# Adding the skip term inside PSUM: a seed matmul ahead of the kernel sums in place of a GpSimd addition

## The chip, the cores and the metric

The kernel runs on one core of a Trainium2 chip. The metric is the device time of one launch in microseconds (us), as the median of several runs. The engines have short names in the profile: PE is TensorE (PEld its weight loads), DVE is VectorE, ACT is ScalarE, POOL is GpSimd, SP is SyncE. A q behind a name (SPq, ACTq, POOLq) is that engine's sequencer, which also issues DMAs.

## The reference

The input `A_u` has 2048 tokens of 448 channels. With `xn` its layer norm, the output is `A_u + A(xn) + B(xn)`.

- `A` is a diagonal state space layer. From five small parameter arrays it builds for each channel d a convolution kernel `K[d, l] = 2 Re sum_n C[d,n] exp(A[d,n] dt[d] l)` over 256 states n and 2048 positions l, convolves `xn` with it through transforms of length 4096, and adds the skip term:

```
y = irfft(rfft(u_t, 2L) * rfft(K, 2L))[:, :, :L]
return y + u * D_skip
```

- `B` is a gated unit: `(sigmoid(xn w_gate) * (xn w_up)) w_down`, 448 to 1792 and back.

A skip term `u * D_skip` is the same as adding `D_skip[d]` to the first tap `K[d, 0]` of the convolution kernel. The kernel uses that, before and after the change.

## The kernel before, in words

Two generators, `conv()` and `glu()`, issue the two halves of the work piece by piece; each `yield` returns a weight, and the loop at the end of the kernel resumes the one that is further behind its total. The program order that comes out is a priority, not yet the order on the engines. `TileContext(schedule_with_timeline_sim=True)` plays the program against a model of the chip ahead of the launch, and puts on each engine's queue the ready instruction of the highest priority; `hp(HP)` raises the priority of what is under it and `tc.issue_after(x)` keeps an instruction behind `x` on its engine. On the chip each queue then runs in that fixed order.

**The gated unit** (`gate`, L689, and `glu`, L724) splits each fp32 operand into a high and a low fp32r part. A tile of 128 hidden units takes 11 matmuls (L703) each for gate and up; the down projection (L816) takes three matmuls for each hidden tile and block of tokens. Weight parts `wh`, `wl` and `dh`, `dl` are made by ACT and DVE in the first half (L753 to L757, L779) with `dl` by POOL (L780); in the second half some are made by POOL (L763, L764, L787, L788). The first `wl` (L755) reads a column of the small tile `lim`, which POOL sets in `limits` (L174 to L176) behind the layer norm's scales.

**The convolution** goes in stages. `prep` (L341) turns the parameters into phases and powers with ACT and DVE. `kgen` (L457) makes the convolution kernel in 56 chunks of 8 channels. For a chunk, POOL builds magnitudes `me` and `mf` by repeated products (`magnitudes`, L493, called for two chunks at a time; L504, L516), ACT squares some of them (L529) and makes cosines and sines `S` (`ahead`, L531) out of a phase matmul (L538), DVE multiplies both into `Et` and `Ft` (L598 to L600), and PE sums over the states with 32 small fp32 matmuls (L612, two passes each in the trace), each into 32 rows and 64 columns of the PSUM tile `ko`.

Four chunks fill one `ko` bank, so there are 14 banks. `ko` has a single buffer. Behind the fourth chunk ACT copies the bank to `ks` in SBUF (L622), and POOL adds the skip weights `dm` to the columns that hold tap 0 (L623). Three chunks later, or at once for the last bank, `first_stage` (L550) multiplies `ks` with a table (L562) and stores the result for `spectra`. In `ko` the four 32-row groups j hold four channels of a slot, and row 32 j, column 0 of slot s holds tap 0; `dm` is therefore zero but for rows 0, 32, 64 and 96, which four small loads fill at the start (L1066, L1067). POOL takes its queue strictly in order, so an addition that waits for its copy keeps the magnitudes behind it waiting too.

`spectra` (L838) then transforms, multiplies and transforms back, beside the second half of the gated unit.

Of the kernel before, what the change touches and what calls it, by code (L numbers as in the profile page):

```python
# [11 lines left out]
F32 = mybir.dt.float32  # L12
F32R = mybir.dt.float32r
I32 = mybir.dt.int32
AF = mybir.ActivationFunctionType
ALU = mybir.AluOpType
# [4 lines left out]
D = 448  # L21
# [34 lines left out]
def _tables():  # L56

    a = np.arange(NA)[:, None]
    k1 = np.arange(NK1)[None, :]
    ang = 2 * np.pi * ((a * k1) % 64) / 64.0  # L60


    wk = np.zeros((4, NA, 2, 2, 32))

    wx = np.zeros((4, NA, 64))
    for j in range(4):
        wk[j, :, 0, j % 2] = np.cos(ang)[:, :32]
        wk[j, :, 1, j % 2] = -np.sin(ang)[:, :32]
        wk[j, :, 1, j % 2, 0] = np.cos(ang)[:, 32]
        wx[j, :, :NK1] = np.cos(ang)  # L70
        wx[j, :, NK1:] = -np.sin(ang)[:, 1:32]
    b = np.arange(NB)[:, None]
    k2 = np.arange(64)[None, :]
    tab = np.zeros((NK1, 128, 128))
    bk = np.zeros((2, 2, 64, 2, 128))
    for q in range(NK1):
        al = 2 * np.pi * ((b * (q + 64 * k2)) % 4096) / 4096.0
        c, s = np.cos(al), np.sin(al)
        tab[q] = np.block([[c, -s], [s, c]])
        if q in (0, 32):  # L80


            for h in range(2):

                split = lambda t: t.reshape(64, 2, 32).transpose(0, 2, 1)
                both = lambda r, i: np.stack([split(r), split(i)], 3).reshape(64, 128)
                bk[q // 32, h, :, 0] = both(c.T, s.T)
                bk[q // 32, h, :, 1] = both(-s.T, c.T)

    tab[0, 64:] = 0.0  # L90
    t32 = np.concatenate([tab[32][:, None], bk[1].reshape(128, 2, 128)], 1)
    tab = tab[:32].reshape(8, 4, 128, 128).transpose(0, 2, 1, 3)

    wf = np.zeros((2, 2, 4, 8, 32, NA))
    for k in range(32):
        ang = 2 * np.pi * ((k * (64 * np.arange(NA)[None] + np.arange(64)[:, None])) % 4096) / 4096.0
        re = (1.0 if k == 0 else 2.0) / 4096.0 * np.cos(ang)
        im = -2.0 / 4096.0 * np.sin(ang)
        if k == 0:
            im = np.broadcast_to(np.cos(np.pi * np.arange(NA))[None] / 4096.0, im.shape)  # L100
        wf[:, 0, k % 4, k // 4] = re.reshape(2, 32, NA)
        wf[:, 1, k % 4, k // 4] = im.reshape(2, 32, NA)

    sel = np.zeros((4, 32, 2, DC, 32))
    st = np.arange(32) + 0.5
    for e in range(DC):
        g, r = e // 2, 6 * (e % 2)  # L110
        for at, sg in ((r, 1.0), (r + 14, -1.0)):
            sel[g, at : at + 2, 0, e] = sg * st
            sel[g, at + 2 : at + 4, 1, e] = sg * st
            sel[g, at + 4 : at + 6, 1, e] = sg
        sel[g, 12, :, e] = MAGIC
        sel[g, 13, :, e] = -MAGIC
    f = lambda v, s: np.ascontiguousarray(v.reshape(s).astype(np.float32))
    return {
        "c_wk": f(wk, (128, 2, 64)),
        "c_wx": f(wx, (128, 64)),  # L120
        "c_tab": f(tab, (8, 128, 4, 128)),
        "c_t32": f(t32, (128, 3, 128)),
        "c_bk": f(bk[0], (128, 2, 128)),
        "c_wf": f(wf, (128, 32, NA)),
        "c_sel": f(sel, (128, 512)),
        "c_id": np.eye(128, dtype=np.float32),
    }

# [2 lines left out]
def s4d_glu_kernel(ctx, tc, io):  # L131
    nc = tc.nc
# [18 lines left out]
    const = ctx.enter_context(tc.tile_pool(name="const", bufs=1, side="left"))  # L151
# [8 lines left out]
    qpi = const.tile([128, 1], F32, name="qpi")  # L160
    nc.gpsimd.memset(qpi, math.pi / 4)

    dm = const.tile([128, D // 32, 8], F32, name="dm")
    nc.gpsimd.memset(dm, 0.0)
    ys = const.tile([128, 16], F32, name="ys")
    zs = const.tile([128, 16], F32, name="zs")
    junk = const.tile([128, 1], F32, name="junk")
# [277 lines left out]
    def powers(pms, g, behind=None):  # L445

        w = W1s[0][:, NCH * g : NCH * g + NCH].rearrange("p g h e -> p (g h e)")
        pm = pms[g % 2]
        with tc.issue_after(behind.ins) if behind else nullcontext():
            nc.scalar.activation(pm[:, 0], w, AF.Identity, bias=one)  # L450
        for j in (1, 2, 3, 4, 5, 7, 8, 9, 10, 11):
            v.scalar_tensor_tensor(pm[:, j], w, 2.0, w, ALU.add, ALU.mult)
            w = pm[:, j]
        for o in (slice(1, 6), slice(7, 12)):
            nc.scalar.activation(pm[:, o], pm[:, o], AF.Identity, bias=one)

    def kgen(pk):  # L457
# [73 lines left out]
        def ahead(cn):  # L531


            S = tl[f"S{cn % 2}"]
            ps = psc[-1].tile([128, 2, 512], F32, name="tr", bufs=1)
            ph = pht[cn // 2 % 2]
            for h in range(2):
                nc.tensor.matmul(ps[:, h], ph[:, cn % 2, 128 * h : 128 * h + 128], sel, start=True, stop=True)  # L538
            if cn % 2 == 1 and cn + 3 < NCK:
                phase_load(cn // 2 + 2)  # L540
            rows = lambda t: t.rearrange("p c (h e) s -> p h c (e s)", h=2)
            pv = ps.rearrange("p h (c x) -> p h c x", c=2)
            cs = S[:, 1:4:2]
            nc.scalar.activation(rows(cs), pv, AF.Abs)  # L544
            nc.scalar.activation(rows(S[:, 0:5:4]), pv, AF.Sin, scale=TWO_PI)
            nc.scalar.activation(rows(S[:, 2:3]), pv[:, :, 0:1], AF.Sin, scale=-TWO_PI)
            sins[:] = [nc.scalar.activation(cs, cs, AF.Sin, scale=-TWO_PI, bias=hpi)]  # L547
            return S
# [33 lines left out]
        for g in range(NCK // NCH):  # L582
            for c in range(NCH):
                cn = g * NCH + c
                S = nxt
                me, mf = (m[:, 2 * DC * (c % 2) : 2 * DC * (c % 2) + 2 * DC] for m in mags)
                if c == 4 and NCH * (g + 1) < NCK:
                    with tc.issue_after(fts[0].ins):
                        powers(pms, g + 1, sins[0])
                if cn + 1 < NCK:  # L590
                    nxt = ahead(cn + 1)
                    if c % 2 == 1:
                        squares(coming[0])
                yield WK / 2
                Et = tl[f"Et{cn % 2}"]
                Ft = tl["Ft"]
                two = lambda ap: ap.unsqueeze(1).to_broadcast([128, 2, 2 * DC, 32])
                v.tensor_tensor(Et[:, :, :, 32:64], two(me[:, :, 32:64]), S[:, 1::-1], ALU.mult)  # L598
                v.tensor_tensor(Et[:, :, :, 0:32], two(me[:, :, 0:32]), S[:, 1:3, :, ::-1], ALU.mult)  # L599
                fts[:] = [v.tensor_tensor(Ft, two(mf), S[:, 3:5], ALU.mult)]  # L600
                if cn + 2 < NCK and c % 2 == 0:
                    coming = magnitudes(cn // 2 + 1)
                if c % 2 == 1:
                    mags = coming
                if cn % 4 == 0:
                    ko = psc[-1].tile([128, 8, 64], F32, name="ko", bufs=1)
                for q in range(2):
                    sl = 2 * (cn % 4) + q
                    for k in range(4):
                        h, cc = k // 2, k % 2  # L610
                        for j in range(4):
                            mm = nc.tensor.matmul(  # L612
                                ko[32 * j : 32 * j + 32, sl],
                                Ft[:, cc, DC * h + 4 * q + j],
                                Et[:, cc, DC * h + 4 * q + j],
                                start=(k == 0),
                                stop=(k == 3),
                                skip_group_check=True,
                            )
                if cn % 4 == 3:  # L620
                    ks = tl["ks"]
                    nc.scalar.copy(ks, ko)  # L622
                    nc.gpsimd.tensor_tensor(ks[:, :, 0], ks[:, :, 0], dm[:, cn // 4], ALU.add)  # L623
                yield WK / 2
                if cn % 4 == 2 and cn > 3 or cn + 1 == NCK:

                    with hp(HP) if cn + 1 == NCK else tc.issue_after(glu_mm[0].ins):
                        first_stage((cn - 3) // 4 if cn + 1 < NCK else cn // 4)
# [387 lines left out]
    def conv():  # L1016
        with tc.tile_pool(name="psk", bufs=1, space=PSUM) as ps_, tc.tile_pool(
            name="pq", bufs=1, side="right"
# [8 lines left out]
            with tc.tile_pool(name="pst", bufs=1, side="right", reuse_waits="tile") as pst:  # L1027
# [35 lines left out]
                nc.sync.dma_start(wk, io["c_wk"])  # L1063
                nc.sync.dma_start(wx, io["c_wx"])
                skip = io["A_D_skip"].rearrange("(g s j) -> j g s", j=4, s=8)
                for j in range(4):  # L1066
                    nc.gpsimd.dma_start(dm[32 * j : 32 * j + 1], skip[j : j + 1])  # L1067
                preps = [prep(pst, h, srcs[h]) for h in range(2)]

                with tc.issue_after(xls[0].ins):  # L1070
# [44 lines left out]
    while any(g is not None for g in gens):  # L1115
# [3 lines left out]
        i = min(live, key=lambda i: done[i] / total[i])  # L1119
# [33 lines left out]
```

## Time and profile before

| | |
|---|---|
| median of 3 runs | 725.41 us (724.01 to 725.96) |
| profiled execution, device time | 727.18 us |
| its span | 725.4 us |
| granted TensorE clock, mean | 0.984 |
| busy: PE, DVE, ACT, POOL | 669.3, 558.1, 428.4, 365.7 us |

The span runs from the first to the last instruction of the profiled execution; the device time has 1.8 us more around it. Busy times are sums over a queue and say nothing about what a stage waits for. A line of a timeline has the start in us, the time that one instruction (or a run of equal ones) took, the engine, the line of the code, the operation, output and input tiles, and in brackets how long the engine had been idle and what ended that. In a table of groups the number behind x is the count, then come busy us and mean ns of one, then the idle time ahead of them. Matmuls are pipelined: the next one starts while the one before still drains, so the cost of one is read from start to start.

### The profile page before, as it was taken

The numbers are of one execution on the slowest core, as the hardware profiler recorded it, in microseconds if no ns is written. First come the engines' busy times: TensorE is split into PE (matmuls) and PEld (weight loads), VectorE is DVE, ScalarE is ACT, GpSimd is POOL, SyncE is SP. The second block draws the span as 40 slices with busy tenths as digits, with TensorE's granted clock in tenths as the row PEclk, the third lists the DMA queues.
The fourth block names the chain that finished last, engine by engine and source line by source line (L and its number), as shares of the span: only waits on it lengthen the run. The fifth ranks groups of instructions, "written<-read, shape, count | busy, mean of one in ns | idle before, by whom it ended". The sixth has DMA issues, their size and how long they took to land.

```text
span 725.4 us, 19184 instructions
## 1 busy us (share of the span) xinstructions
PE 669.3 (92%) x7752; PEld 525.6 (72%) x7752; DVE 558.1 (77%) x766; ACT 428.4 (59%) x678; POOL 365.7 (50%) x431
## 2 busy tenths in 40 slices
PE   2797999999997996998999999999999999998995
PEld 2666888887876873656788778887777787666783
DVE  5899897599899889897878888987946555545543
ACT  3655975578788777975777777777642322312320
POOL 2100138566987975796666688577843002250001
PEclk9999999999999998999999999999999999999998
DMA  9957184454254443656833334141369999999745
GB/s 205 238 142 226 38 253 141 149 166 148 67 168 141 133 121 111 173 147 200 256 101 101 98 110 147 45 143 42 82 173 321 231 238 225 247 263 215 183 121 160
DMA packets 102984, 117.24 MB, mean 162 GB/s; under 512 B 13232, under 2 KB 90864, under 8 KB 102896
## 3 DMA queue, kind: packets, MB, share of 16 engines
q1 hardware_dynamic: 78736, 91.87, 46.9%
q10 hardware_dynamic: 21584, 18.24, 9.4%
q0 software_dynamic: 2576, 5.90, 3.0%
q8 instruction: 61, 1.00, 0.6%
q14 instruction: 27, 0.22, 0.1%
HBM read 72.13 MB, written 43.84 MB: 160 GB/s over the span
## 4 chain that ended last, share of the span: by engine, by line
PE 63%; DVE 13%; DMA 8%; ACT 6%; issue 4%; SPq 3%; POOL 2%; ACTq 0%; POOLq 0%; DVEq 0%
PE gu L703 27%; PE po L816 14%; PE sp L898 7%; PE ko L612 6%; PE pv L925 4%; PE tr L538 4%; DVE Ft L600 2%; DVE Et L598 2%; DMA sx<-x_d 2%; DVE Et L599 2%; DMA ph<-ph_d 1%; PE kp L562 1%; DMA xe<-in_A_u_dram 1%; ACT S L547 1%; DVE hl L721 1%
## 5 line engine op out<-in xcount | busy, mean ns | idle before, releaser
L516 POOL TENSOR_TENSOR me<-me,pm 128x32 f32<-128x32 f32 (+1 forms) x168 | 141.6, 843 | 77.7 <-DVE Et L599 66.7
L516 POOL TENSOR_TENSOR mf<-mf,pm 128x64 f32<-128x64 f32 (+1 forms) x112 | 116.5, 1040 | 5.9
L703 PE MATMUL gu<-xh,wh 128*128 128x512 f32 x336 | 98.6, 401 | 1.6 <-ACT xh L221 0.7
L703 PE MATMUL gu<-xh,wl 128*128 128x512 f32 x336 | 96.0, 391 | 0.0
L703 PE MATMUL gu<-xl,wh 128*128 128x512 f32 x336 | 95.5, 390 | 0.0
L598 DVE TENSOR_TENSOR Et<-me,S 128x1024 f32<-128x1024 f32 x56 | 84.5, 1509 | 13.7 <-ACT S L547 12.8
L816 PE MATMUL po<-dh,hh 128*128 128x448 f32 x224 | 84.3, 377 | 6.3 <-DVE hf L714 4.4
L599 DVE TENSOR_TENSOR Et<-me,S 128x1024 f32<-128x1024 f32 x56 | 79.2, 1414 | 11.4 <-ACT me L529 9.3
L600 DVE TENSOR_TENSOR Ft<-mf,S 128x1024 f32<-128x1024 f32 x56 | 79.5, 1420 | 6.4 <-PE ko L612 3.3
L816 PE MATMUL po<-dl,hh 128*128 128x448 f32 x224 | 82.7, 369 | 0.0
L816 PE MATMUL po<-dh,hl 128*128 128x448 f32 x224 | 81.7, 368 | 0.0
L544 ACT ACTIVATE S<-tr 128x1024 f32<-128x1024 f32 x56 | 57.6, 1029 | 38.7 <-PE tr L538 38.4
L612 PEld LDWEIGHTS ko<-Et,Ft 128*32 128x32 f32 x3584 | 54.7, 111 | 31.4 <-issue 12.9
L719 ACT CAST hh<-hf 128x512 fp32r<-128x512 f32 x56 | 34.9, 624 | 69.8 <-DVE hf L714 69.6
L703 PEld LDWEIGHTS gu<-xh,wh 128*128 128x128 f32 x336 | 60.6, 188 | 21.1 <-issue 4.4
L612 PE MATMUL ko<-Et,Ft 128*32 128x64 f32 x3584 | 65.1, 223 | 10.9 <-DVE Ft L600 9.8
L703 PEld LDWEIGHTS gu<-xh,wl 128*128 128x128 f32 x336 | 62.9, 188 | 14.2 <-DVE ve L256 0.7
L703 PEld LDWEIGHTS gu<-xl,wh 128*128 128x128 f32 x336 | 62.9, 188 | 13.3
L714 DVE SCALAR_TENSOR_TENSOR hf<-th,gu 128x512 f32<-128x512 f32 x56 | 38.0, 679 | 40.2 <-PE gu L703 25.7
L780 POOL TENSOR_TENSOR dl<-rd,dh 128x448 fp32r<-128x448 f32 x14 | 23.5, 1679 | 84.6 <-ACT dh L779 84.6
L547 ACT ACTIVATE S<-S,hpi 128x1024 f32<-128x1024 f32 x56 | 65.5, 1170 | 0.0
L821 DVE SCALAR_TENSOR_TENSOR acc<-po,acc 128x448 f32<-128x448 f32 x80 | 48.1, 616 | 21.3 <-PE po L816 21.2
(208 smaller groups left out, 1304.2 us busy)
## 6 DMA issues: line engine op xcount, KB each, us to landing
sk_d<-sk ACTq DMA_DIRECT2D x14, 512.0 KB
sx<-x_d SPq DMA_DIRECT2D x32, 224.0 KB
skl<-sk_d SPq DMA_DIRECT2D x16, 448.0 KB
vp<-v_d SPq DMA_DIRECT2D x16, 448.0 KB
v_d<-vt SPq DMA_DIRECT2D x62, 112.0 KB
ph<-ph_d SPq DMA_DIRECT2D x224, 24.0 KB
wt_d<-wh SPq DMA_DIRECT2D x9, 512.0 KB
wt_d<-wl SPq DMA_DIRECT2D x9, 512.0 KB
```

The source lines that it names most:

```text
L516: ins = nc.gpsimd.tensor_tensor(m[:, :, w + a : 2 * w : n], m[:, :, a:w:n], par(base + i).unsqueeze(2).to_broadcast([128, 4 * DC, w // n]) ...
L544: nc.scalar.activation(rows(cs), pv, AF.Abs)
L547: sins[:] = [nc.scalar.activation(cs, cs, AF.Sin, scale=-TWO_PI, bias=hpi)]
L598: v.tensor_tensor(Et[:, :, :, 32:64], two(me[:, :, 32:64]), S[:, 1::-1], ALU.mult)
L599: v.tensor_tensor(Et[:, :, :, 0:32], two(me[:, :, 0:32]), S[:, 1:3, :, ::-1], ALU.mult)
L600: fts[:] = [v.tensor_tensor(Ft, two(mf), S[:, 3:5], ALU.mult)]
L612: mm = nc.tensor.matmul(ko[32 * j : 32 * j + 32, sl], Ft[:, cc, DC * h + 4 * q + j], Et[:, cc, DC * h + 4 * q + j], start=(k == 0), stop=( ...
L703: glu_mm[:] = [nc.tensor.matmul(ps, a_, b_, start=(n == 0), stop=(n == len(mm) - 1))]
L714: marks[1] = v.scalar_tensor_tensor(hf, th, 1.0, pgu[1], ALU.add, ALU.mult)
L816: glu_mm[:] = [nc.tensor.matmul(po, a_[:, bs], w_, start=(n == 0), stop=(n == 3 * fc - 1))]
L821: v.scalar_tensor_tensor(acc[:, b], po, 0.5, acc[:, b], ALU.mult, ALU.add)
L898: mm = nc.tensor.matmul(to, tb[:kk, t, 64 * c : 64 * c + 64], rhs, start=True, stop=True, skip_group_check=True,)
```

## The change

The skip weights are no longer added to `ks`. Ahead of a bank's first chunk, one fp32r matmul with the 0/1 table `pick` as weights and a 128 x 16 slice of `dm` as moving operand opens the bank (`start=True`) and writes columns 0 and 1 of all eight slots. The 128 matmuls of the four chunks then all accumulate (`start=False`).

`dm` now holds each skip weight as three fp32r parts whose sum is exact: the rounded value in rows 0 to 3, the rounded remainder in rows 32 to 35, the rest in rows 64 to 67; `pick` sums the three and puts channel group j on row 32 j. The parts are made at the start by POOL: three loads of the same 4 x 112 weights into `d0`, and a chain of copies (which round to fp32r) and subtractions.

```
--- before
+++ after
+    pick = np.zeros((128, 4, 32))
+    for j in range(4):
+        pick[j:96:32, j, 0] = 1.0
...
+        "c_pick": f(pick, (128, 128)),
...
-    dm = const.tile([128, D // 32, 8], F32, name="dm")
-    nc.gpsimd.memset(dm, 0.0)
+    dm = const.tile([128, D // 32, 8, 2], F32R, name="dm")
+    nc.gpsimd.memset(dm.bitcast(F32), 0.0)
+    pick = const.tile([128, 128], F32R, name="pick")
...
                 if cn % 4 == 0:
                     ko = psc[-1].tile([128, 8, 64], F32, name="ko", bufs=1)
+                    nc.tensor.matmul(
+                        ko[:, :, 0:2], pick, dm[:, cn // 4], start=True, stop=False, skip_group_check=True
+                    )
...
-                                start=(k == 0),
+                                start=False,
...
                     nc.scalar.copy(ks, ko)
-                    nc.gpsimd.tensor_tensor(ks[:, :, 0], ks[:, :, 0], dm[:, cn // 4], ALU.add)
...
                 skip = io["A_D_skip"].rearrange("(g s j) -> j g s", j=4, s=8)
-                for j in range(4):
-                    nc.gpsimd.dma_start(dm[32 * j : 32 * j + 1], skip[j : j + 1])
+                nc.gpsimd.dma_start(pick, io["c_pick"])
+                d0, d1 = (pst.tile([128, D // 32, 8], F32, name=f"d{i}") for i in range(2))
+                dr = pst.tile([128, D // 32, 8], F32R, name="dr")
+                nc.gpsimd.memset(d0, 0.0)
+                for i in range(3):
+                    nc.gpsimd.dma_start(d0[32 * i : 32 * i + 4], skip)
+                nc.gpsimd.tensor_copy(dm[0:32, :, :, 0], d0[0:32])
+                for i, (a_, b_) in enumerate(((d0, d1), (d1, d0))):
+                    rs = slice(32 * i + 32, 32 * i + 64)
+                    nc.gpsimd.tensor_copy(dr, a_)
+                    nc.gpsimd.tensor_tensor(b_, a_, dr, ALU.subtract)
+                    nc.gpsimd.tensor_copy(dm[rs, :, :, 0], b_[rs])
```

## The prediction

> **What bounds the kernel now.** I read the busy shares first, then the chain of work that ended last, then a table of three stretches: up to the first kernel sum, the 56 chunks, and the rest.
>
> ```profile
> PE 669.3 (92%) x7752; PEld 525.6 (72%) x7752; DVE 558.1 (77%) x766; ACT 428.4 (59%) x678; POOL 365.7 (50%) x431
> PE 63%; DVE 13%; DMA 8%; ACT 6%; issue 4%; SPq 3%; POOL 2%; ACTq 0%; POOLq 0%; DVEq 0%
> 0.00:126.80 126.80, 105.45 (x525) 85.12 (x525) 108.36 (x214) 79.33 (x145) 33.07 (x55) 0.99 0.68 177
> 126.80:534.00 407.20, 385.42 (x5753) 305.01 (x5752) 351.47 (x364) 302.25 (x445) 293.81 (x329) 0.99 0.44 131
> ```
>
> In the last two lines the columns are the stretch, its length, busy us of PE, PEld, DVE, ACT and POOL, granted clock, DMA share and GB/s. In the 407.2 us of the chunks PE is busy for 385.4, or 95%, and idle for 21.8; PE has 63% of the chain, POOL 2%. So time that goes from POOL's queue is worth something only where PE, or DVE ahead of it, waits for POOL, and a matmul that is added costs nearly what it occupies.
>
> Next, who waits around the step that goes, and for whom POOL waits.
>
> ```profile
> L623 POOL TENSOR_TENSOR ks<-ks,dm 128x8 f32<-128x8 f32 x14 | 11.2, 799 | 10.4 <-ACT ks L622 10.4
> PE kp L562 <- POOL ks L623: 1.2, 1, 1.2
> POOL me L516 <- DVE Et L599: 66.7, 20, 5.8
> DVE Et L599 <- POOL me L516: 2.1, 1, 2.1
> PE ko L612 <- DVE Ft L600: 9.8, 10, 3.4
> ```
>
> The 14 additions take 11.2 us of POOL and hold its queue for 10.4 us more while they wait for the copy. PE waits for them once, 1.2 us. But POOL itself waits 66.7 us, in 20 places, until DVE has read the magnitudes of two chunks before; DVE waits for POOL once, 2.1 us. POOL is ahead almost everywhere, and time freed there mostly lengthens that wait.
>
> **The change part by part.**
>
> *1. The additions go.* Behind most of them POOL was idle next anyway. I looked in POOL's timeline at what follows each of the 14. Four have work right behind them:
>
> ```profile
> 194.35 1.19 POOL L623 TENSOR_TENSOR ks<-ks,dm 128x8 f32<-128x8 f32 x1
> 313.93 1.19 POOL L623 TENSOR_TENSOR ks<-ks,dm 128x8 f32<-128x8 f32 x1
> 512.68 1.19 POOL L623 TENSOR_TENSOR ks<-ks,dm 128x8 f32<-128x8 f32 x1
> 533.19 0.58 ACT L622 COPY ks<-ko 128x512 f32<-128x512 f32 x1
> 533.85 0.22 POOL L623 TENSOR_TENSOR ks<-ks,dm 128x8 f32<-128x8 f32 x1 [0.90 <-ACT ks L622]
> 534.04 2.37 POOL L764 TENSOR_TENSOR wl<-wraw,wh 128x1024 fp32r<-128x1024 f32 x1
> 534.13 0.27 PE L562 MATMUL kp<-wk,ks 64*64 64x64 f32 x1 [1.25 <-POOL ks L623]
> ```
>
> At the last bank the gain is plain: the copy ends at 533.77, the first-stage matmul starts at 534.13, and without the addition it can start some 0.05 us behind the copy, so **-0.3 us**. What is late next there is the copy itself. At the other three POOL is 1.19 us early afterwards. The bounds for POOL's part are 0 and all four, 3 x 1.19 + 0.22 + 0.90 = 4.7 us; with one wait of DVE on POOL in the whole run I take **-0.3 us** beside the last bank's.
>
> *2. One matmul for each bank comes.* The trace has no matmul with 128 x 128 weights and 16 moving columns. The nearest rows are the 128 x 128 transposes at the full clock, which also load 128 columns of weights for a short stream, and the last wide matmul ahead of a chunk:
>
> ```profile
> 25.11 0.27 PE L212 MATMUL tr<-ident,xn 128*128 128x128 f32 x1
> 25.21 0.27 PE L212 MATMUL ko<-ident,xn 128*128 128x128 f32 x1
> 159.05 0.39 PE L703 MATMUL gu<-xr,wl 128*128 128x512 f32 x1
> 159.28 0.39 PE L703 MATMUL gu<-xl,wh 128*128 128x512 f32 x1
> 159.60 1.10 PE L612 MATMUL ko<-Et,Ft 128*32 128x64 f32 x64
> ```
>
> Transposes start 0.10 us apart. Wide matmuls start 0.23 us apart, yet from the last one to the chunk there are 0.32, so changing from wide weights to the 32-column ones costs 0.09. That change is paid today; but today the chunk's first weights load beside a matmul of 512 columns, and behind the seed they would have 16 columns as cover. So I charge 0.10 for the seed and the 0.09 a second time: 0.19, say 0.2 us. Bounds: 0 if all of it fits in a gap, and 0.45 if it costs a whole wide weight load (188 ns in the profile) and a whole transpose (0.27). Below nothing it can't be. In two banks PE was idle for DVE's `Ft` ahead of the first chunk, 0.35 and 0.46 us, and there the seed hides:
>
> ```profile
> 223.37 1.10 PE L612 MATMUL ko<-Et,Ft 128*32 128x64 f32 x64 [0.35 <-DVE Ft L600]
> 513.95 1.10 PE L612 MATMUL ko<-Et,Ft 128*32 128x64 f32 x64 [0.46 <-DVE Ft L600]
> L703 PEld LDWEIGHTS gu<-xh,wl 128*128 128x128 f32 x336 | 62.9, 188 | 14.2 <-DVE ve L256 0.7
> ```
>
> 12 x 0.2 = **+2.4 us**, from 0 to 12 x 0.45 = 5.4. The Trainium skill, "TensorE: Matmul & The Clock Gate", section "LDWEIGHTS (loading the stationary operand)", gives columns / 1.2 ns, 107 ns here, and "Step-by-step: what each phase is for" says that a load is pulled ahead beside the matmul that runs. By that a load is free only while a long enough matmul covers it, which speaks against a 16-column one; 12 x 107 ns would make +1.3 us, an estimate from that page. The 0.10 us from transpose to transpose agrees with it.
>
> The 3584 passes of L612 stay as many and as long; that they accumulate instead of overwriting I cost at nothing.
>
> *3. A wait moves.* The seed needs the bank free, so it waits for the copy L622 as the first chunk's matmul did. It doesn't need `Et` and `Ft`, so the plan may put it earlier on PE's queue, and there everything behind it, the wide matmuls above all, would wait with it. Four of the later banks show the room, each by its last matmul, its copy, or the next bank's first matmul:
>
> ```profile
> 215.37 1.10 PE L612 MATMUL ko<-Et,Ft 128*32 128x64 f32 x64
> 220.86 0.57 ACT L622 COPY ks<-ko 128x512 f32<-128x512 f32 x1
> 307.65 0.60 ACT L622 COPY ks<-ko 128x512 f32<-128x512 f32 x1
> 309.66 0.54 PE L612 MATMUL ko<-Et,Ft 128*32 128x64 f32 x24
> 330.94 0.42 PE L612 MATMUL ko<-Et,Ft 128*32 128x64 f32 x14
> 344.75 0.58 ACT L622 COPY ks<-ko 128x512 f32<-128x512 f32 x1
> 349.81 0.38 PE L612 MATMUL ko<-Et,Ft 128*32 128x64 f32 x12
> 450.70 1.10 PE L612 MATMUL ko<-Et,Ft 128*32 128x64 f32 x64
> 455.45 0.56 ACT L622 COPY ks<-ko 128x512 f32<-128x512 f32 x1
> ```
>
> The smallest distance from a copy's end to the next bank's first matmul, over all 13, is 309.66 - 308.25 = 1.4 us. The seed follows a `yield` in the program, so the gated unit's matmuls issued before it have the higher priority and it should land close to its chunk. I take **0**; the other end is the first rival.
>
> *4. The start.* Four loads of 112 weights go, and the load of `pick` and three loads of 448 come in their place on POOL's queue, with a clear of `d0` before and seven small operations behind.
>
> ```profile
> 2.10 2.14 POOL L1067 DMA_DIRECT2D dm<-in_A_D_skip_dram  x4
> 11.97 0.10 POOL L174 MEMSET lim<- 128x3 f32 x1 [7.72 <-DVE zs L263]
> 12.80 1.28 DVE L755 SCALAR_TENSOR_TENSOR wl<-wraw,lim,wh 128x1024 fp32r<-128x1024 f32 x1
> 23.95 0.34 POOL L1061 CAST sel<-zs 128x1 fp32r<-128x1 f32 x1
> dm<-in_A_D_skip_dram POOLq DMA_DIRECT2D x4, 0.4 KB, 5.3
> sel<-in_c_sel_dram POOLq DMA_DIRECT2D x1, 256.0 KB, 9.3
> ```
>
> Four loads leave in 2.14 us today; for the clear and four times as many pieces in each load I add 0.8 us, an estimate, and let the last one leave at 5 us. With 5.3 us to land it is there at 10.3. Seven operations at 0.34 (the small cast's row) are 2.4 us, so POOL is done at 12.7 if they stand ahead of `lim`, 0.7 us late for it; `wl` on DVE starts 0.8 us behind `lim` today and may slip as much. POOL's idle 7.7 us cover the rest. Bounds: 0, if the plan puts `lim` first, and the late landing priced below as a rival. I take **+0.5 us**. The seed's first use is at 126.8 us, far behind. `dm`'s wider clear, the added SBUF and the tables cost nothing on a path: POOL's idle time hides the clear, and no instruction moves the rest.
>
> **Sum:** -0.3 - 0.3 + 2.4 + 0 + 0.5 = +2.3 us. Against the profiled execution's own 727.18 us that is 729.5. It ran 1.77 us above the median of the runs shown, so the forecast for the median is 725.41 + 2.3 = **727.7 us**.
>
> **The rivals.**
>
> *A seed that waits* (733.7). In six of the first 13 banks the copy ends more than 3 us behind the bank's last matmul: the rows above have the first (221.43 against 216.47), the widest (345.33 against 331.36) and the last (456.01 against 451.80). If the plan thinks the copy earlier than the chip has it and puts the seed forward, PE stalls. At 1 us in each of the six: 2.3 + 6 = +8.3. For it: the seed is ready before its chunk. Against: the gated unit's priority. It decides when the seed stands over 1.4 us ahead of its chunk.
>
> *POOL was in the way after all* (721.4, the other side). The chain's 2% for POOL have runs of magnitudes:
>
> ```profile
> 270.64 1.29 POOL me L516
> 272.00 1.17 POOL me L516
> ```
>
> If the chunks behind the four additions with work behind them are waited for, all 4.7 us come off. With the seed at 12 x 0.06 (a third of the 0.2, the rest in gaps) and nothing at the start: -4.7 + 0.7 = -4.0. It decides where DVE reaches `Et` before the magnitudes are done. For it: one 2.1 us wait of DVE on POOL, and 21.6 us of queue freed. Against: POOL's 66.7 us of waiting for DVE.
>
> *A late start* (732.0). The load of `sel` took 9.3 us to land. If the three small-element loads take that, they are there at 14.3, POOL is done at 16.7, and `lim`, `wl` and all behind it on DVE slip by 4.8 us: 2.3 - 0.5 + 4.8 = +6.6. It decides if the plan has the seven operations ahead of `lim`. The Trainium skill, "DMA: Bandwidth & Descriptors", section "Why a DMA increments its semaphore by 16 and not by 1", says that a transfer is spread over as many engines as divide its slowest dimension; four rows make four engines, which is this rival's case. The trace shows 5.3 us for one-row loads and no four-row load.
>
> *Nothing visible* (725.5): the seeds hide in PE's 21.8 us of gaps and POOL's gain is nil.
>
> That the addition stays can't be; L623 is gone from the code.
>
> **How the numbers follow.** About 0.3%, 2.2 us, is what a measurement of this kernel can tell from no change. Forecast 0.38 (a quarter of it under +2.2), POOL in the way 0.30, the waiting seed 0.12, the late start 0.10, nothing visible 0.10. The plan is made anew with 28 instructions exchanged, so each case has a few us of its own around it; that gives faster 0.28, same 0.22, slower 0.50. The range goes from a little below the POOL case to a little above the waiting seed, 720.5 to 735.0.
>
> **What would show it.** Right: the seed's row with its start 0.1 to 0.3 us ahead of the chunk's, the first-stage matmul of the last bank 0.3 us earlier behind its copy, POOL's wait for `Et` longer by some 15 to 20 us, no new wait on L622. Wrong: PE waiting for ACT `ks` at the seed; `lim` and L755 later than 13.5 us; or POOL's `me` gone from the chain and the chunks shorter.

## The result, and the profile after

The changed kernel takes 736.8 us (median of 4 runs, 729.9 to 738.7) against 725.7 us for the kernel before beside it: a ratio of 1.0155 [1.0113, 1.0196], 11 us slower. In the last series below, with more runs on another chip, it is 1.0167 [1.0139, 1.0195]. The profiled execution took 735.11 us with a span of 733.3 us; runs of any of these kernels spread over 1 to 1.5%, so small differences are read from intervals and from the traces.

The page of the changed kernel, busy times and then the chain by engine:

```profile
PE 677.9 (92%) x7766; PEld 531.4 (72%) x7766; DVE 552.6 (75%) x766; ACT 429.7 (59%) x678; POOL 357.5 (49%) x425
PE 66%; DVE 12%; DMA 9%; ACT 5%; issue 3%; SPq 2%; POOL 1%; ACTq 1%; POOLq 0%; DVEq 0%
```

PE has 14 matmuls more and is busy 8.6 us more. The same three stretches as before, up to the first chunk, to the last bank's copy, and the rest:

```profile
0.00:132.05 132.05, 106.00 (x526) 85.77 (x526) 108.62 (x214) 79.41 (x145) 37.64 (x64) 0.97 0.71 171
132.05:546.00 413.95, 394.93 (x5766) 310.54 (x5765) 346.19 (x363) 302.89 (x445) 280.95 (x315) 0.97 0.44 129
546.00:733.30 187.30, 176.99 (x1476) 135.05 (x1476) 97.79 (x189) 47.36 (x91) 38.86 (x48) 0.99 0.89 221
```

The first chunk starts at 132.05 us, 5.25 later than the 126.80 of before. Taken to the start of the last bank's copy in both (545.97 and 533.19 us), the chunks take 413.9 us against 406.4, and the rest is 4.9 us shorter. So two losses have to be explained, one ahead of any seed and one among the chunks.

Among the chunks PE does not wait longer than before. By the rows it is idle for 413.95 - 394.93 = 19.0 us, where the prediction counted 21.8. It is busy 9.5 us longer, with 13 matmuls more and at a granted clock of 0.97 in place of 0.99. From these two figures an estimate of what the clock is worth is 385.42 x 0.99 / 0.97 - 385.42 = 7.9 us, a rough one, because the clock has two digits only.

**The start.** POOL's and ACT's timeline of the changed kernel, from the three loads to the first `wh` and `wl`:

```profile
3.17 3.14 POOL L1078 DMA_DIRECT2D d<-in_A_D_skip_dram  x3 [0.30 <-POOL d L1076]
15.41 0.28 POOL L1082 CAST dr<-d 128x112 fp32r<-128x112 f32 x1 [4.09 <-DMA d<-in_A_D_skip_dram]
15.69 1.28 ACT L760 ACT_TABLE_LOAD   x1 [15.69 <-DMA wraw<-in_B_w_up_dram]
16.99 1.04 ACT L760 CAST wh<-wraw 128x1024 fp32r<-128x1024 f32 x1
17.30 0.10 POOL L179 MEMSET lim<- 128x3 f32 x1
18.13 1.28 DVE L762 SCALAR_TENSOR_TENSOR wl<-wraw,lim,wh 128x1024 fp32r<-128x1024 f32 x1 [5.74 <-ACT wh L760]
```

The last of the loads lands at 15.4 us, not at 10.3, and `lim` is set at 17.3 instead of 12.0, as the rival of the late start had it. But the row of `wl` names something else: it waited for `wh`, and ACT had waited until 15.69 us for the raw weights, which SP's queue loads. In the kernel before, that cast ran at 11.07. Two causes would fit, and they fall on nearly the same moment: a late `lim`, or late weights.

**The seeds.** The waits of PE and POOL in the changed kernel (total us, times, longest):

```profile
PE ko L620 <- DVE Ft L605: 9.2, 7, 3.7
PE ko L612 <- ACT ks L630: 4.1, 2, 3.5
POOL me L521 <- DVE Et L604: 82.8, 16, 10.7
```

L612 is the seed. PE now waits at two seeds for the copy of the bank before, 4.1 us by this view. POOL waits 82.8 us for `Et` instead of 66.7: the time freed there became waiting.

### The profile page after: what moved, and what is told of

Same layout as the page of the kernel before. It is cut to its first block, busy times and chain, and to the rows that moved or that the text cites. A ratio compares the mean times of both kernels' runs of the same rounds, so it can differ in the third digit from the quotient of the medians.

```text
span 733.3 us, 19227 instructions
## 1 busy us (share of the span) xinstructions
PE 677.9 (92%) x7766; PEld 531.4 (72%) x7766; DVE 552.6 (75%) x766; ACT 429.7 (59%) x678; POOL 357.5 (49%) x425
## 4 chain that ended last, share of the span: by engine, by line
PE 66%; DVE 12%; DMA 9%; ACT 5%; issue 3%; SPq 2%; POOL 1%; ACTq 1%; POOLq 0%; DVEq 0%
PE gu L710 26%; PE po L823 16%; PE sp L905 6%; PE ko L620 6%; PE tr L543 4%; PE pv L932 4%; DMA sx<-x_d 2%; DVE Ft L605 2%; DMA wraw<-in_B_w_gate_dram 2%; DVE Et L603 2%; DVE Et L604 1%; DMA xe<-in_A_u_dram 1%; PE gu L286 1%; DMA raw<-in_B_w_gate_dram 1%; PE kp L567 1%
## 5 line engine op out<-in xcount | busy, mean ns | idle before, releaser
L521 POOL TENSOR_TENSOR me<-me,pm 128x32 f32<-128x32 f32 (+1 forms) x168 | 144.1, 858 | 100.8 <-DVE Et L604 82.8
L521 POOL TENSOR_TENSOR mf<-mf,pm 128x64 f32<-128x64 f32 (+1 forms) x112 | 114.0, 1018 | 5.3
L710 PE MATMUL gu<-xh,wh 128*128 128x512 f32 x336 | 101.4, 407 | 1.3 <-ACT xh L226 0.8
L603 DVE TENSOR_TENSOR Et<-me,S 128x1024 f32<-128x1024 f32 x56 | 82.6, 1476 | 16.1 <-ACT S L552 14.9
L604 DVE TENSOR_TENSOR Et<-me,S 128x1024 f32<-128x1024 f32 x56 | 78.3, 1398 | 13.4 <-ACT me L534 9.7
L787 POOL TENSOR_TENSOR dl<-rd,dh 128x448 fp32r<-128x448 f32 x14 | 25.4, 1816 | 87.6 <-ACT dh L786 87.6
```

The source lines that it names most:

```text
L521: ins = nc.gpsimd.tensor_tensor(m[:, :, w + a : 2 * w : n], m[:, :, a:w:n], par(base + i).unsqueeze(2).to_broadcast([128, 4 * DC, w // n]) ...
L710: glu_mm[:] = [nc.tensor.matmul(ps, a_, b_, start=(n == 0), stop=(n == len(mm) - 1))]
```

## The experiments

**Theories.** For the start: (1) the three loads of 4 x 112 scattered values, 1344 pieces of four bytes, hold the DMA engines, and the weights come late; against it (2), POOL's chain of small operations holds back `lim`. For the chunks: (3) a seed placed early on PE's queue waits there for the copy, and what stands behind it waits too; against it (4), taking the additions away gives a worse order of the queues, or (5) the seeds' own matmuls are dear.

### Preparation held until later

```
+    dls.append(nc.gpsimd.tensor_tensor(dl, rd, dh, ALU.subtract))
...
+    if n == 1:
+        with tc.issue_after(dls[-1].ins):
+            (pick, d0, the loads and the chain, moved here)
```

> The changed kernel with the whole preparation of the skip parts (the table, the three loads, the POOL chain) kept behind one of POOL's low-part subtractions some tens of us into the run. In the changed kernel's profile the first chunk starts at 132.1 us instead of 126.8. Theory 1 (the three loads of four-byte pieces hold the DMA engines at the start) and theory 2 (POOL's chain holds back lim) both expect the first wh cast back near 11 us and the first chunk within 1 us of 126.8. Theory 3 (the seeds and a new order of the queues cost the rest, in the chunks) expects the total to stay 2 to 5 us above the kernel before, 728 to 731; if the start carries all of it, 726.

Measured: 1.0135 [1.0063, 1.0207]; the first `wh` cast at 10.68 us, the first chunk at 128.3 in the profile. That is 1.5 us behind the kernel before, and two kernels below whose start is unchanged have the first chunk at 127.4 and 128.4, so the start is mended. The total is still over 1% up, by the medians 11 us where 2 to 5 were expected: the start doesn't carry all of it, and what is left is more than was expected.

### Only `lim` ahead of POOL's chain

```
+    lims.append(nc.gpsimd.memset(lim[:, i, 2:3], -87.0))
...
+    with tc.issue_after(lims[0].ins):
         nc.gpsimd.tensor_copy(dm[0:32, :, :, 0], d0[0:32])
         ...
```

> The changed kernel with only POOL's seven small operations held behind the first setting of lim; the three loads stay at the very start. Theory 1 (DMA engines held by four-byte pieces): the first wh cast still waits for its weights until about 17 us, the first chunk stays at 131 to 132 us, the total near 735. Theory 2 (POOL's queue order): lim is set at 12 us, the first chunk is back at 127, the total near 730.

Measured: 1.0197 [1.0125, 1.0269]; the first chunk at 133.0 us. This kernel's timeline at the start:

```profile
12.07 0.10 POOL L179 MEMSET lim<- 128x3 f32 x1 [5.76 <-DVE zs L268]
16.00 1.28 ACT L760 ACT_TABLE_LOAD   x1 [16.00 <-DMA wraw<-in_B_w_up_dram]
17.29 1.04 ACT L760 CAST wh<-wraw 128x1024 fp32r<-128x1024 f32 x1
```

`lim` is set at 12.07, when it was before, and nothing else moves: the weights still come at 16. Theory 2 falls.

### The same loads, neighbouring values

```
-    nc.gpsimd.dma_start(d0[32 * i : 32 * i + 4], skip)
+    nc.gpsimd.dma_start(d0[32 * i : 32 * i + 4], flat)      # flat: (j g s) -> j g s
```

> The changed kernel with the three loads reading 112 neighbouring values for each row instead of every fourth value: same bytes, rows, queue and POOL work, but the skip weights land on the wrong channels. Theory 1: 12 long pieces instead of 1344 of four bytes, so the loads land in 5 to 6 us, the first wh cast is back near 11 us, the first chunk at 127 to 128, the total near 730. If it is not the size of the pieces but the loads and the table as such, the first chunk stays at 131 to 132 us.

Measured: 1.0112 [1.0043, 1.018]; the first chunk at 127.9 us. Its timeline:

```profile
3.19 1.52 POOL L1079 DMA_DIRECT2D d<-in_A_D_skip_dram  x3 [0.29 <-POOL d L1076]
8.38 0.27 POOL L1080 CAST dm<-d 32x112 fp32r<-32x112 f32 x1 [3.67 <-DMA d<-in_A_D_skip_dram]
11.12 1.04 ACT L760 CAST wh<-wraw 128x1024 fp32r<-128x1024 f32 x1
```

The same bytes on the same queue in long pieces, and `wh` is back at 11.1. (The skip weights land on the wrong channels here, so the output is not the reference's.) So it is the size of the pieces: theory 1. What they do is seen in 6 to 10 us, in the DMA view (packets, MB, share of 16 engines). The kernel before, the changed one, and then the stretch of this experiment, whose last two columns are DMA share and GB/s:

```profile
q1 hardware_dynamic: 1095, 0.79, 106.8%
q0 software_dynamic: 52, 0.00, 1.5%
```

```profile
q1 hardware_dynamic: 643, 0.30, 141.9%
q0 software_dynamic: 151, 0.04, 21.0%
```

```profile
6.00:10.00 4.00, 0.00 (x0) 0.00 (x0) 2.13 (x9) 0.17 (x1) 1.13 (x4) 1.00 0.98 203
```

q1 is SP's queue with the weights, q0 POOL's. POOL's own packets take only 21% of the engines, yet SP's move 0.30 MB instead of 0.79: one of its packets takes 1.419 x 16 x 4 us / 643 = 141 ns in place of 1.068 x 16 x 4 us / 1095 = 62. The engines show as busy while they move little, and whoever shares them pays.

### The start without the seeds

```
+    dz = const.tile([128, 8], F32, name="dz")     # zeros
-    nc.gpsimd.tensor_tensor(ks[:, :, 0], ks[:, :, 0], dm[:, cn // 4], ALU.add)
+    nc.gpsimd.tensor_tensor(ks[:, :, 0], ks[:, :, 0], dz, ALU.add)
     (and the change's preparation in place of the four loads)
```

> The kernel before with the new preparation at the start but without the seeds: POOL still adds to the kernel sums, a tile of zeros, so the skip term is left out. Theory 1 or 2: the first chunk at 131 to 132 us, the total 4 to 6 us above the kernel before, 730 to 732. Theory 3 alone (the cost is in the chunks): the total within 1 us of the kernel before.

This kernel adds zeros and leaves the skip term out. Measured: 1.0089 [1.0048, 1.0131], 6 us; the first chunk at 132.06. The start alone costs that, about half of the whole.

### No addition, no seed

```
-    nc.gpsimd.tensor_tensor(ks[:, :, 0], ks[:, :, 0], dm[:, cn // 4], ALU.add)
```

> The kernel before with only POOL's 14 additions taken out (the skip term is left out); loads and start as before, no seed. If POOL's queue was in the way, the total falls by 2 to 5 us. If POOL's freed time only lengthens its waits, within 2 us of the kernel before. If the missing additions alone bring a worse order of the queues, in the chunks around the change of halves (bank 6 to 7, 37 us before, 43 us with the change), the total rises by 3 us or more.

This kernel too leaves the skip term out. Measured: 0.9993 [0.9953, 1.0033]. The waits of its POOL and DVE:

```profile
POOL me L516 <- DVE Et L599: 72.1, 19, 9.0
DVE Et L599 <- POOL me L516: 1.4, 1, 1.4
```

Within the interval, 3.4 us down and 2.4 up, nothing is gained by freeing POOL, nor does the new order that comes of it cost anything. Theory 4 falls, at least for a price of 3 us or more, and so does the rival by which POOL was in the way and 4.7 us would come off.

### Seeds of zeros, additions kept

```
+    nc.tensor.matmul(ko[:, :, 0:2], zr, zr[:, 0:16].rearrange("p (s i) -> p s i", s=8),
+                     start=True, stop=False, skip_group_check=True)
...
-    start=(k == 0),
+    start=False,
```

> The kernel before with a seed of zeros ahead of each bank, everything accumulating onto it, and POOL's additions kept as they are; start as before. If the seeds are the cost in the chunks (0.11 us each from start to start, 1.5 us, and 4 to 5 us of waits for the copy), the total is 5 to 8 us above the kernel before and bank 6 to 7 takes 41 us or more. If the missing additions bring it, within 2 us.

Measured: 1.0058 [1.0018, 1.0099], 4 us. PE's waits:

```profile
PE ko L609 <- ACT ks L628: 4.6, 2, 3.6
```

The seeds bring their wait, and a cost, without any change to POOL's work or the start. It is less than the 5 to 8 us expected. 0.89% for the start, 0.58% for the seeds and nothing for the additions make 1.47%, against 1.55% and 1.67% measured for the whole change; each of the parts has an interval of some 0.4 points to either side.

### A hold that held nothing

```
+    with tc.issue_after(glu_mm[0].ins):
         nc.tensor.matmul(ko[:, :, 0:2], pick, dm[:, cn // 4], start=True, stop=False, ...)
```

> The changed kernel with the preparation held until later and each seed kept on PE's queue behind the gated unit's matmuls that the program issued before it, so that it stands next to its chunk. If a seed put forward on the queue is the cost: no wait of PE for the copy over 0.5 us, the total 3 to 6 us below the kernel with the late preparation. If not: the same total, 731 to 735.

The edit is made to the kernel with the late preparation. Measured: 1.0074 [1.0036, 1.0112], with 4.8 us of PE waiting at the seeds as in the first run of that kernel. The edge names the gated unit's last matmul issued so far in program order; the seed still got its early place, so this run says nothing on what that place costs.

### The seed next to its chunk

```
+    tc.add_manual_dep(sd.ins, fts[0].ins.name,        # sd: the seed, fts[0]: the chunk's Ft
+        mybir.DependencyInfo(mybir.DependencyClass.Sync, mybir.DependencyReason.DATA), reason="seed")
```

on the kernel with the late preparation, beside that kernel, the changed one and the next one on one chip:

> The changed kernel with the late preparation, where each seed also waits for its chunk's Ft, as the chunk's own matmuls do, so that it stands next to them on PE's queue. If the seeds' early places are the cost: no wait of PE for the copy, and the total 3 to 6 us below the kernel with the late preparation beside it, close to the one with the seed behind the chunks. If a seed ahead of a bank costs by itself (its own matmul, the order that it brings): no more than 1.5 us below.

> The changed kernel as it is, beside the three others on one chip. Start and seeds add up: 1.3 to 1.7% above the kernel before; 5 us above the kernel with the late preparation.

> The kernel with the late preparation once more, on one chip with the others: 0.6 to 0.9% above the kernel before if the seeds alone are left (the kernel with seeds and additions had 0.58%).

| one chip | median, us | ratio to before |
|---|---|---|
| the kernel before | 725.0 | |
| the change | 736.2 | 1.0167 [1.0139, 1.0195] |
| preparation late | 731.4 | 1.0124 [1.0088, 1.0160] |
| late, seed behind the four chunks | 727.7 | 1.0058 [1.0031, 1.0085] |
| late, seed next to its chunk | 726.4 | 1.0021 [0.9993, 1.0049] |

The ratios are the recorded ones; the quotient of two medians can differ from them by some tenths of a per cent (731.4 / 725.0 is 1.009). The kernel with the late preparation came out above the 0.6 to 0.9% that were expected of it by its ratio, and at the upper end by its median.

Waiting for `Ft` sounds like one wait more; by the ratios it takes 1.0 point off, and by the medians 5.0 us, which is 0.7%. PE's timeline at two of the banks, first in the changed kernel, then in this one:

```profile
226.40 0.39 PE L710 MATMUL gu<-xl,wh 128*128 128x512 f32 x1
227.35 0.28 PE L612 MATMUL ko<-dm,pick 128*128 128x16 f32 x1 [0.56 <-ACT ks L630]
227.49 0.70 PE L710 MATMUL gu<-xl,wh 128*128 128x512 f32 x2
287.12 0.28 PE L612 MATMUL ko<-dm,pick 128*128 128x16 f32 x1 [3.49 <-ACT ks L630]
288.06 1.67 PE L620 MATMUL ko<-Et,Ft 128*32 128x64 f32 x64 [0.66 <-DVE Et L603]
```

```profile
223.60 0.84 PE L714 MATMUL gu<-xh,wh 128*128 128x512 f32 x3
224.76 0.25 PE L612 MATMUL ko<-dm,pick 128*128 128x16 f32 x1 [0.32 <-DVE Ft L605]
224.94 1.10 PE L624 MATMUL ko<-Et,Ft 128*32 128x64 f32 x64
280.67 0.97 PE L286 MATMUL gu<-xt,wx 32*64 32x448 f32 x4 [2.93 <-DVE hf L725]
281.57 0.86 PE L543 MATMUL tr<-sel,ph 128*128 128x512 f32 x2
282.22 0.21 PE L612 MATMUL ko<-dm,pick 128*128 128x16 f32 x1
282.37 1.06 PE L624 MATMUL ko<-Et,Ft 128*32 128x64 f32 x26
```

At 227 the early seed cuts a group of gate matmuls in two and makes the second part wait 0.56 us for a copy it has nothing to do with. At 287 nothing runs on PE for 3.5 us, until the copy has come. Next to its chunk the seed waits for no copy in the whole run. The seed's place is what costs: theory 3 holds in that, and theory 5 is settled by what is left, 0.21% [-0.07, 0.49].

That the two waits are the price does not follow. At 287 the bank's own chunk stands next behind the seed; it needs the same copy, and then waits 0.66 us more for `Et`. And PE pauses at this point without an early seed too, for DVE's `hf`: 2.9 us in the kernel with the seed next to its chunk (280.67 above), and in the kernel before

```profile
283.13 1.76 PE L281 MATMUL gu<-xt,wx 32*64 32x448 f32 x4 [5.51 <-DVE hf L714]
```

What differs is seen from the copy of bank 5 to that of bank 8, around the change of halves. The kernel before takes 369.86 - 280.28 = 89.6 us, the one with the seed next to its chunk 369.95 - 279.67 = 90.3, the late kernel 377.95 - 282.24 = 95.7. In this order, with the columns as above:

```profile
280.28:369.86 89.58, 82.97 (x1246) 57.81 (x1247) 74.16 (x84) 68.67 (x112) 61.71 (x74) 0.96 0.62 175
279.67:369.95 90.28, 85.75 (x1249) 60.20 (x1250) 72.77 (x82) 68.78 (x111) 66.18 (x74) 0.92 0.60 173
282.24:377.95 95.71, 90.19 (x1251) 61.57 (x1252) 69.74 (x82) 71.78 (x115) 47.93 (x70) 0.89 0.56 162
```

PE is idle for 6.6, 4.5 and 5.5 us in them, and runs nearly the same number of matmuls. So of the 5.4 us between the last two, 1.0 is idle time and 4.4 are matmuls that take longer, at a lower granted clock. Busy time multiplied by the clock is nearly the same in all three, 80, 79 and 80 us. Between these two copies the clock is 0.86 to 0.89 in all eight traces with a seed put early, and 0.92 to 0.96 in the six others. Whether the waits at the seeds or the different order of the queues lowers the clock was not separated.

### The seed behind the four chunks

```
+    start=(cn % 4 == q == k == 0),      # in place of start=False
...
                 if cn % 4 == 3:
+    nc.tensor.matmul(ko[:, :, 0:2], pick, dm[:, cn // 4], start=False, stop=True, ...)
```

> The changed kernel with the preparation held until later, and with the seed matmul behind a bank's fourth chunk instead of ahead of its first: the first matmul of each 32-row group of the bank starts it, all others accumulate, the seed closes it. The seed then waits for no copy. If the waits of PE at the seeds (4.8 us in the profile of the kernel with the late preparation) are the cost in the chunks: those waits are gone and the total is 4 to 6 us below that kernel, 727 to 729. If the cost is the new order of the queues, which the missing additions or the seeds bring whatever the place: the total stays at 731 to 735.

> The kernel with the late preparation and the seed behind the fourth chunk once more, on one chip with the others: 3 to 5 us below the kernel with the late preparation if PE's waits at the seeds are the price, the same within 1.5 us if the new order is.

Measured: 1.0033 [0.9995, 1.0071] on the chip of the kernels without additions and with seeds of zeros, 1.0058 [1.0031, 1.0085] in the table above, 3.7 us below the late kernel. PE waits for no copy at these seeds either. That agrees with theory 3 as to the place, by another edit. No version was clearly faster than the kernel before; the one without additions shows that there was little or nothing on POOL to be had.

## Why the prediction was wrong, point by point

The sign was right; the time lies above the range. Two of the signs named for being wrong came: PE waits for ACT's `ks` at a seed, and `lim` and the first `wl` (17.3 and 18.1 us) are later than 13.5.

- **What bounds the kernel:** right. POOL is ahead, and freed time lengthens its wait for `Et`: 82.8 us from 66.7, 16 us, where 15 to 20 were named.
- **1, the additions go (-0.6 us in all):** right within what was measured, 0.9993 [0.9953, 1.0033]. In the changed kernel the last bank's copy ends and the first-stage matmul starts 0.05 us on, as forecast:

```profile
545.97 0.58 ACT L630 COPY ks<-ko 128x512 f32<-128x512 f32 x1
546.60 0.27 PE L567 MATMUL kp<-wk,ks 64*64 64x64 f32 x1 [0.94 <-ACT ks L630]
```

- **2, the seeds' own time (+2.4 us):** too high. A seed among the down projection's matmuls of the changed kernel:

```profile
170.51 0.36 PE L823 MATMUL po<-dh,hl 128*128 128x448 f32 x1
170.71 0.37 PE L823 MATMUL po<-dh,hh 128*128 128x448 f32 x1
170.92 0.17 PE L612 MATMUL ko<-dm,pick 128*128 128x16 f32 x1
170.94 0.45 PE L823 MATMUL po<-dl,hh 128*128 128x448 f32 x1
171.23 0.37 PE L823 MATMUL po<-dh,hl 128*128 128x448 f32 x1
```

  These start 0.205 us apart. From 170.71 to 171.23 there are two of them and the seed, 0.52 us: the seed adds 0.11, 1.5 us for 14. The first term of 0.10 was right; the second change of weights, 0.09, isn't paid. By the Trainium skill, "TensorE: Matmul & The Clock Gate", section "LDWEIGHTS (loading the stationary operand)", a weight load takes columns / 1.2 ns, which makes 107 ns for the 128 columns of `pick`, an estimate from that page. The price from start to start is close to that, but the load's own rows in this trace last 188 ns (median of 14). Next to its chunk, where the prediction had the seed, even the 0.11 doesn't show. With the seed moved there, there are 0.32 us from the last wide matmul to the chunk with the seed in between, the same as the 0.32 without one that the prediction read from 159.28 and 159.60:

```profile
194.86 0.39 PE L714 MATMUL gu<-xh,wh 128*128 128x512 f32 x1
195.08 0.17 PE L612 MATMUL ko<-dm,pick 128*128 128x16 f32 x1
195.18 1.10 PE L624 MATMUL ko<-Et,Ft 128*32 128x64 f32 x64
```

- **3, the wait that moves (taken as 0):** the step that failed among the chunks. It reasoned that the gated unit's matmuls, issued earlier in the program, would keep the seed near its chunk. In the changed kernel 11 of 14 seeds have gated-unit matmuls right behind them, and two seeds wait for the copy. The early place costs 5 us by medians on one chip. The rival saw the place coming but priced it as six stalls of 1 us; there were two, of 3.5 and 0.6 us, and PE's idle time among the chunks did not grow (19.0 us, 21.8 before). In the traces most of the price is matmuls that take longer at a lower granted clock, a term that neither the sum nor the rival had.
- **4, the start (+0.5 us):** the step that failed at the start, in mechanism and size. The rival of the late start had the slow landing right (9.3 us priced; the row of the changed kernel's loads has the same median) and the 5 us, but put them on `lim`. With `lim` set in time nothing was gained. The loads' landing was taken as a matter for POOL alone; what counted was what they did to the weights on SP's queue:

```profile
d<-in_A_D_skip_dram POOLq DMA_DIRECT2D x3, 1.8 KB, 9.3
```

  The prediction counted the pieces, three times 448 in place of four times 112, for the time that POOL takes to issue them, and left out what they do to the transfers of others, in a stretch where the first cast waits for SP's loads.
- **The sum:** +2.3 us, with two rivals at +8.3 and +6.6 taken as alternatives. They were not alternatives: one lies at the start and one among the chunks, and they came together. Their prices above the shared terms are 6.0 for the seeds and 4.3 for the start, and 2.3 + 6.0 + 4.3 = +12.6 us stands close to the 11 us measured. That closeness is partly luck, since neither price came in the way that it was worked out. The range ended at the dearer one alone.

From the last bank's copy on, the changed kernel's trace takes 187.3 us, the kernel's before 192.2 and that of the start alone 190.6. What makes it shorter with the seeds stays open.

## What to carry to other kernels

An instruction that opens a buffer needs less than the work it opens for, so a planned queue may put it forward: give it its successor's wait, or do the step last. Read what a place costs from the stretch's idle time, busy time and granted clock, and not from the length of the wait that stands out. Count a load's pieces as well as its bytes, and look at whose transfers share the engines at that time. Rivals that sit in different stages add up; the range has to hold their sum.

## What was not expected of the hardware

Three loads of 5.4 KB together, in 1344 pieces of four bytes, took the DMA engines' throughput in 6 to 10 us from 201 to 86 GB/s, while the share of time that the engines show as busy rose:

```profile
6.00:10.00 4.00, 0.00 (x0) 0.00 (x0) 2.09 (x10) 0.23 (x1) 0.00 (x0) 1.00 1.10 201
```

```profile
6.00:10.00 4.00, 0.00 (x0) 0.00 (x0) 2.57 (x13) 0.00 (x0) 0.32 (x1) 1.00 1.64 86
```

The first row is the kernel before, the second the changed one (the last two columns are DMA share and GB/s). The Trainium skill, "DMA: Bandwidth & Descriptors", section "Why small descriptors are slow (HBM only)", has a fixed cost for each descriptor. That such pieces on one queue also more than double the time of another queue's packets, 62 to 141 ns, is this trace's. Two more kernels with these loads at the start, the one with `lim` first and the one with the start alone, moved 89 and 75 GB/s in the same 4 us.
